# Another order of the first steps in a fused window-attention and MLP kernel

## The chip, the cores and the metric

The kernel runs on one core of a Trainium2 chip. The metric is the device time of one execution in microseconds (us); several executions give a median. One execution is also recorded by the hardware profiler, and its trace is what is read below. The engines are called PE (TensorE, matmuls), DVE (VectorE), ACT (ScalarE), POOL (GpSimd) and SP (SyncE, which here only issues transfers); "PEld" is TensorE's weight load and "POOLq", "SPq", "ACTq" are the issues of transfers on the queues of these engines.

## The reference

An attention with a sliding window and a few sink positions is followed by a two-layer MLP with a rational activation. Cut to what matters:

```python
# q, k, v: (4, 8, 768, 64) float32; n_sink 4, window 128
scores = q @ k.T / sqrt(64), kept where key < 4 or 0 <= query - key < 128
x = softmax(scores) @ v                     # heads side by side: (3072, 512)
h = x @ w_in                                # (3072, 2048)
P = a0 + a1*h + a2*h**2 + a3*h**3
Q = 1 + |b0|*|h| + |b1|*h**2
out = (P / Q) @ w_out                       # (3072, 512)
```

## The kernel before

The work is cut into 12 steps of 256 rows (4 batches of 3 steps). Each step has an attention part and an MLP part. Everything is a named "piece" with an engine; ORDER, a hand-written list of piece numbers, says in which order all pieces are issued, and so each engine's queue: every engine works through its own pieces in that order and waits at the head of its queue until the inputs of the piece are there. ENGINE says for pieces that can go to ScalarE or VectorE which one takes them, BANK which of four PSUM tiles (ps_h, ps_o, ps_m, ps_s, two banks each) a piece writes. Each of these tiles exists once, so a piece that writes ps_h waits until the reader of its previous contents is done.

The pieces, with s the step (or m in the MLP):

- Step 0's k and q: load_k0 and load_q0 (two halves, on the ACT and SP queues, in float32), cast_k0 and cast_q0 (to bf16), turn_k0 and turn_q0 (TensorE transposes into PSUM), place_k0 and place_qc 0 (copies out of PSUM).
- Steps 1 to 3: load_kc and load_qc (POOL's queue, cast in flight), turn_kc and turn_qc, place_kc and place_qc. Steps 0 to 2 have load_vc, turn_vc and place_vc for v in the same way; turn_vc multiplies with the selection tile "sel", which is made of the identity.
- From step 4 on k and q go through POOL's load_k and load_q and through DMA transposes on SP's queue, turn_k and turn_q. v goes through load_v, one for each head.
- scores s i (four parts), exps s i (ScalarE), attend s G (two parts), norm s G (a reciprocal and a multiplication on VectorE), turn_x and placed_x, which give x transposed.
- gemm1 m j (four parts of x @ w_in), copy_in m j (ScalarE), then on VectorE and ScalarE and, sqa or sqd (square), den, ln, exp, even, odd, odd_h, num and gate, then gemm2 m (w_out) and copy_out, store. Step 0 does this chain in four quarters.
- hold x s and hold h m: a one-element copy on POOL that reads the norm of step s (or the hidden rows of step m), so that the loads behind it on POOL's queue are issued only then.
- Small things: "neg" and "edges" (mask tiles), "ident", sink_consts, spread, cast_vs, turn_vs, spread_vs (sink rows of v), babs (on ScalarE) and scale_x and scalars (on VectorE; the norms multiply with what scale_x gives), clear_* and ones_* (fills), spin n (n matmuls of 128 columns on a constant tile, which compute nothing that is used).

The dependency that the list keeps is in the calls of piece(); for example the norm:

```python
piece(("norm", s, G), "DVE", 0.97, 4 * s + at - 5 - 0.1,
      lambda s=s, G=G: normalize(s, G),
      [("attend", s, G), ("scale_x",), ...
```

The order is written out by hand, and the last loop of the kernel issues it:

```python
names = list(work)
for n in ORDER:
    if n < 0:
        spin(-n)
    elif work[names[n]].run:
        work[names[n]].run()
```

Of the kernel before, what the change touches and what calls it, by code (L numbers as in the profile page):

```python
# [61 lines left out]
def kernel(  # L62
# [50 lines left out]
    inv_sqrt_d = 1.0 / float(D) ** 0.5  # L113
    NEG = -30000.0
    PE_MASK = tuple(range(12))
    ENGINE = {('cast_q0', 0): 'DVE',
               ('cast_q0', 1): 'DVE',
               ('place_k0', 1): 'ACT',
               ('place_kc', 2, None): 'ACT',
# [1148 lines left out]
```

## Time and profile before

| | us |
|---|---|
| median of 3 runs | 242.64 (241.71 to 242.86) |
| the profiled execution | 240.56 |
| its span, from the first to the last instruction | 238.9 |

| engine | busy us | share of the span | instructions |
|---|---|---|---|
| PE | 216.1 | 90% | 3229 |
| DVE | 215.2 | 90% | 253 |
| ACT | 210.1 | 88% | 172 |
| POOL | 92.7 | 39% | 126 |

A timeline row gives the start in us, the duration in us, the engine, the line of the kernel, the operation and its tiles, how many instructions are merged in it, and in brackets how long the engine was idle before it and what released it. A row of transfers gives the tile, the queue, the number of issues, the size and the time from the issue to the landing.

### The profile page before, as it was taken

Reading aid. Unit: us, or ns where it says so; the run is one execution under the profiler, and the core shown is the slowest. Engines: PE = TensorE matmul, PEld = TensorE weight load, DVE = VectorE, ACT = ScalarE, POOL = GpSimd, SP = SyncE. Lnnn points to the kernel's source line nnn. Section 1 sums busy time; section 2 is a strip of 40 time slices with the busy share of each in tenths; the row PEclk is TensorE's granted clock in tenths of the full one; section 3 lists DMA queues with packets and bytes.
Section 4 is the critical chain, followed back from the end, with each engine's and each line's share of the span. In section 5 each row is a group of like instructions: output and inputs, shape, how many; then the busy total and the mean of one; then the engine's idle time right before and its main releaser. Section 6 shows DMA issues by size and latency. Waiting matters only on the chain.

```text
span 238.9 us, 7308 instructions
## 1 busy us (share of the span) xinstructions
PE 216.1 (90%) x3229; PEld 146.8 (61%) x3249; DVE 215.2 (90%) x253; ACT 210.1 (88%) x172; POOL 92.7 (39%) x126
## 2 busy tenths in 40 slices
PE   0497898995999999999999999999999999999993
PEld 0365676784874757746578658568647768545431
DVE  3678299999799999898999999999999999999991
ACT  2357799997899998999999899999999999999960
POOL 8914409597939880499910980000000000000000
PEclk9999999999999999999999999999999999999999
DMA  6999999999999999799994999570305110004222
GB/s 186 166 178 137 202 170 79 125 134 128 164 185 147 137 162 150 208 98 77 141 129 89 158 89 73 140 125 26 25 3 198 25 25 0 1 3 170 93 88 88
DMA packets 95375, 26.98 MB, mean 113 GB/s; under 512 B 86128, under 2 KB 92272, under 8 KB 95344
## 3 DMA queue, kind: packets, MB, share of 16 engines
q0 software_dynamic: 65024, 12.98, 84.8%
q1 hardware_dynamic: 28792, 12.61, 28.4%
q10 hardware_dynamic: 1528, 0.93, 1.4%
q8 instruction: 25, 0.41, 0.8%
q14 instruction: 6, 0.05, 0.1%
HBM read 27.30 MB, written 6.29 MB: 141 GB/s over the span
## 4 chain that ended last, share of the span: by engine, by line
PE 52%; ACT 24%; DVE 7%; DMA 6%; issue 4%; POOL 4%; SPq 2%; ACTq 0%; POOLq 0%; DVEq 0%
PE ps_h L829 18%; PE ps_o L767 9%; PE ps_m L767 8%; ACT lnq L811 6%; ACT hb L774 5%; ACT den L816 4%; DMA kT<-k_bf 4%; PE ps_m L829 3%; ACT sq L781 3%; ACT e L667 3%; PE ps_h L767 2%; DMA v<-in_v_dram 2%; PE ps_m L708 2%; PE ps_s L647 1%; SPq L602 1%
## 5 line engine op out<-in xcount | busy, mean ns | idle before, releaser
L767 PEld LDWEIGHTS <-w_in_sb 128*128 128x128 bf16 x768 | 73.7, 98 | 14.8 <-issue 3.5
L829 PE MATMUL ps_h<-w_out_sb,g 128*128 128x512 bf16 x287 | 68.2, 379 | 1.9 <-issue 1.0
L829 PEld LDWEIGHTS <-g 128*128 128x128 bf16 x384 | 36.6, 98 | 42.0 <-DVE g L821 1.6
L811 ACT ACTIVATE lnq<-den,one_eps,qsc 128x4096 f32<-128x4096 bf16 (+1 forms) x18 | 48.2, 2678 | 0.0
L816 ACT ACTIVATE den<-lnq 128x4096 bf16<-128x4096 f32 (+1 forms) x18 | 44.8, 2491 | 0.2
L767 PE MATMUL ps_m<-xblk,w_in_sb 128*128 128x256 bf16 x352 | 42.1, 273 | 0.6 <-ACT hb L774 0.3
L767 PE MATMUL ps_o<-xblk,w_in_sb 128*128 128x256 bf16 x336 | 40.2, 273 | 0.0
L381 POOL DMA_DIRECT2D v<-in_v_dram x48 | 36.1, 765 | 0.1
L808 DVE TENSOR_TENSOR num<-num,sq 128x4096 bf16<-128x4096 bf16 (+1 forms) x18 | 28.3, 1578 | 0.2
L821 DVE TENSOR_TENSOR g<-num,den 128x4096 bf16<-128x4096 bf16 (+1 forms) x18 | 28.3, 1574 | 0.1
L805 DVE TENSOR_TENSOR sq<-sq,hb 128x4096 bf16<-128x4096 bf16 (+1 forms) x18 | 28.3, 1576 | 0.1
L792 DVE TENSOR_TENSOR den<-den,sq 128x4096 bf16<-128x4096 bf16 (+1 forms) x18 | 28.2, 1574 | 0.1
L774 ACT ACTIVATE hb<-ps_o 128x1024 bf16<-128x1024 f32 x21 | 21.8, 1038 | 3.3 <-PE ps_o L767 3.2
L774 ACT ACTIVATE hb<-ps_m 128x1024 bf16<-128x1024 f32 x22 | 22.9, 1039 | 0.6 <-PE ps_m L767 0.5
L667 ACT ACTIVATE e<-ps_s 128x768 bf16<-128x768 f32 (+1 forms) x25 | 22.1, 885 | 0.0
L781 ACT ACTIVATE sq<-hb 128x1024 bf16<-128x1024 bf16 (+1 forms) x15 | 20.1, 1355 | 0.1
L797 DVE TENSOR_SCALAR num<-sq,acoef 128x4096 bf16<-128x4096 bf16 (+1 forms) x18 | 18.3, 1024 | 0.4 <-ACT sq L781 0.3
L801 DVE TENSOR_SCALAR sq<-sq,acoef 128x4096 bf16<-128x4096 bf16 (+1 forms) x18 | 17.9, 999 | 0.2
L783 DVE TENSOR_TENSOR sq<-hb 128x2048 bf16<-128x2048 bf16 (+2 forms) x13 | 16.9, 1300 | 1.0 <-ACT hb L774 0.9
L708 PEld LDWEIGHTS <-e 64*64 64x64 bf16 x1216 | 13.1, 107 | 5.4 <-issue 4.4
L343 POOL DMA_DIRECT2D q_bf<-in_q_dram x15 | 14.8, 988 | 3.7 <-DMA w_out_sb<-in_moe_w_out_dram 3.5
L788 DVE TENSOR_SCALAR den<-hb 128x2048 uint32<-128x2048 uint32 (+1 forms) x18 | 16.1, 896 | 0.0
(136 smaller groups left out, 265.8 us busy)
## 6 DMA issues: line engine op xcount, KB each, us to landing
out_dram<-o_t SPq DMA_DIRECT2D x11, 512.0 KB, 3.0
w_in_sb<-in_moe_w_in_dram POOLq DMA_DIRECT2D x4, 512.0 KB, 10.8
k_bf<-in_k_dram POOLq DMA_DIRECT2D x16, 128.0 KB, 6.2
w_out_sb<-in_moe_w_out_dram POOLq DMA_DIRECT2D x4, 512.0 KB, 8.8
q_bf<-in_q_dram POOLq DMA_DIRECT2D x15, 128.0 KB, 6.2
v<-in_v_dram POOLq DMA_DIRECT2D x24, 64.0 KB, 5.8
stage_v<-in_v_dram POOLq DMA_DIRECT2D x3, 256.0 KB, 9.8
v<-in_v_dram POOLq DMA_DIRECT2D x24, 32.0 KB, 5.0
```

What stands on the lines that cost most here:

```text
L381: nc.gpsimd.dma_start(out=v_fix[b % 2][half(r), g * NHF:(g + steps) * NHF, hl, 0:D], in_=v[b, h, g * TS:(g + steps) * TS, :].rearrange("(j ...
L667: nc.scalar.activation(out=data, in_=ps[:, :, c0:512], func=AF.Exp, scale=inv_sqrt_d)
L767: nc.tensor.matmul(ps[:, n, :], lhsT=w_in_all[:, c, fc * P:(fc + 1) * P], rhs=xblk[m][:, c, :], start=(c == 0), stop=(c == NDMC - 1))
L774: nc.scalar.activation(out=hb[m][:, j * GW:(j + 1) * GW], in_=ps_h.pop((m, j)).rearrange("p n c -> p (n c)"), func=AF.Copy)
L781: nc.scalar.activation(out=sq[m][:, c], in_=hb[m][:, c], func=AF.Square)
L792: nc.vector.tensor_tensor(out=den[m][:, c], in0=den[m][:, c], in1=sq[m][:, c], op=ALU.add)
L805: nc.vector.tensor_tensor(out=sq[m][:, c], in0=sq[m][:, c], in1=hb[m][:, c], op=ALU.mult)
L808: nc.vector.tensor_tensor(out=num[m][:, c], in0=num[m][:, c], in1=sq[m][:, c], op=ALU.add)
L811: nc.scalar.activation(out=lnq_fix[:, c], in_=den[m][:, c], func=AF.Ln, scale=qsc, bias=one_eps)
L816: nc.scalar.activation(out=den[m][:, c], in_=lnq_fix[:, c], func=AF.Exp, scale=-1.0)
L821: nc.vector.tensor_tensor(out=g_of[m][:, c], in0=num[m][:, c], in1=den[m][:, c], op=ALU.mult)
L829: nc.tensor.matmul(ps_out[own][:, tt, :], lhsT=g_of[m][:, co:co + P], rhs=w_out_all[:, fc, :], start=(fc == 0), stop=(fc == NFFC - 1))
```

## The change

ORDER is changed in its first 319 entries; from there on the list is the same. The spin of 3 ahead of the first scores becomes a spin of 7 between the two turns of q for step 3. Eight pieces change their engine and some thirty their PSUM tile. The queues of the engines, written out by names as far as they differ (before, after):

```
PE    before  q0 0, k0 1, q0 1, k0 0 (turns), turn_kc 1, spin 3, scores 0 1, scores 0 2, turn_vs 0, turn_qc 1,
              scores 0 3, scores 0 0, turn_vs 1, turn_vc 0, turn_kc 2, attend 0 1, attend 0 0, turn_vc 1, scores 1 0,
              turn_x 0 1, turn_x 0 0, turn_qc 2, scores 1 3, 1 2, 2 2, 2 0, 1 1, gemm1 0 1, attend 1 0, turn_kc 3,
              turn_vc 2, gemm1 0 2, gemm1 0 0, attend 1 1, scores 2 1, turn_qc 3 1, turn_x 1 0, turn_qc 3 0, scores 2 3, ...
      after   q0 1, q0 0, k0 0, k0 1 (turns), turn_qc 1, scores 0 1, turn_kc 1, scores 0 3, turn_vs 1, scores 0 0,
              turn_vc 0, turn_vc 1, turn_vs 0, scores 0 2, turn_kc 2, scores 1 0, attend 0 1, turn_qc 2, attend 0 0,
              scores 2 2, scores 1 3, turn_x 0 1, scores 2 0, scores 1 2, turn_x 0 0, scores 1 1, gemm1 0 1, attend 1 0,
              scores 2 3, turn_vc 2, turn_kc 3, gemm1 0 2, gemm1 0 0, attend 1 1, turn_qc 3 0, spin 7, turn_qc 3 1, ...
ACT   before  (loads), place_qc 0 0, place_qc 0 1, place_k0 1, exps 0 1, 0 2, 0 3, 0 0, place_vc 0, babs, load_a,
              place_kc 2, place_vc 1, exps 1 0, place_qc 2, exps 1 3, 1 2, 2 2, copy_in 0 1, exps 1 1, 2 0, place_kc 3, ...
      after   (loads), load_a, cast_q0 0, place_qc 0 1, place_k0 0, place_k0 1, place_qc 1, exps 0 1, 0 3, place_kc 1,
              exps 0 0, place_vc 1, exps 0 2, babs, exps 1 0, place_qc 2, exps 2 2, 2 0, 1 3, 1 2, 1 1, copy_in 0 1,
              exps 2 3, place_kc 3, place_vc 2, ...
DVE   before  neg, fills, cast_q0 1, sel, fills, ones_vs, spread, cast_k0 1, sink_edge, cast_q0 0, cast_vs 1, cast_k0 0,
              place_k0 0, cast_vs 0, k_sink 0, place_kc 1, ones_v, spread_vs 0, place_qc 1, spread_vs 1, sink_mask 0,
              scale_x, norm 0 1, norm 0 0, placed_x 0 1, placed_x 0 0, scalars, norm 1 0, ..., place_vc 2, ..., norm 1 1
      after   neg, fills, cast_q0 1, cast_k0 1, ones_vs, sel, cast_k0 0, place_qc 0 0, k_sink 0, sink_edge, spread,
              ones_v, cast_vs 1, spread_vs 1, cast_vs 0, place_vc 0, spread_vs 0, sink_mask 0, scale_x, place_kc 2,
              norm 0 1, norm 0 0, placed_x 0 1, scalars, placed_x 0 0, norm 1 0, ..., norm 1 1
POOL  before  edges, sink_consts, load_kc 1, load_qc 1, ident, load_vc 0, load_kc 2, load_vc 1, load_v 3 4, load_kc 3,
              load_qc 2, load_w_in 1, load_vc 2, hold x 0, load_w_in 2, load_w_in 0, load_qc 3, load_w_in 3, load_v 3 1,
              load_k 4 0, load_k 4 1, hold x 1, load_q 9, load_v 4 1, load_k 5 1, load_v 3 7, load_q 10, load_k 5 0,
              load_v 3 6, load_q 11, hold x 2, ...
      after   sink_consts, ident, edges, load_qc 1, load_kc 1, load_vc 0, load_vc 1, load_kc 2, load_v 3 7, load_qc 2,
              load_kc 3, load_w_in 1, load_vc 2, load_w_in 2, hold x 0, load_w_in 0, load_v 3 4, load_v 3 6, load_qc 3,
              load_w_in 3, load_q 11, load_k 4 0, hold x 1, load_q 10, load_v 4 1, load_q 9, load_k 5 1, load_k 4 1,
              load_v 3 1, load_k 5 0, hold x 2, ...
SP    before  ..., turn_k 4 1, turn_q 9, turn_k 5 1, turn_k 4 0, turn_q 10, turn_q 11, turn_k 5 0, ...
      after   ..., turn_k 4 0, turn_q 10, turn_q 9, turn_k 5 1, turn_k 4 1, turn_q 11, turn_k 5 0, ...
```

The diff, with the first lines of ORDER and all else:

```diff
 ORDER = [
-    3, 108, 126, 1, 2, 125, 128, 109, 117, 127, 113, 118, 0, 14, 15, 146, 107, 110, 5, 4, 16, 119,
-    136, 121, 122, 129, 140, 8, 116, 143, 133, 144, 137, 141, 145, 147, 138, 148, 139, 142, 149,
-    130, 178, -3, 182, 150, 184, 183, 131, 185, 120, 151, 132, 24, 186, 152, 180, 18, 187, 181, 17,
...
+    3, 109, 126, 1, 2, 125, 128, 107, 127, 108, 0, 15, 117, 113, 146, 14, 110, 118, 119, 140, 5,
+    147, 111, 136, 122, 4, 8, 143, 148, 16, 144, 137, 145, 138, 139, 121, 141, 151, 142, 178, 182,
+    152, 116, 129, 149, 120, 133, 27, 183, 186, 134, 17, 187, 180, 135, 150, 18, 6, 181, 101, 9,
...
@@ -113,16 +113,16 @@
     inv_sqrt_d = 1.0 / float(D) ** 0.5
     NEG = -30000.0
     PE_MASK = tuple(range(12))
-    ENGINE = {('cast_q0', 0): 'DVE',
-               ('cast_q0', 1): 'DVE',
+    ENGINE = {('cast_q0', 1): 'DVE',
+               ('place_k0', 0): 'ACT',
                ('place_k0', 1): 'ACT',
-               ('place_kc', 2, None): 'ACT',
+               ('place_kc', 1, None): 'ACT',
                ('place_kc', 3, None): 'ACT',
-               ('place_qc', 0, 0): 'ACT',
                ('place_qc', 0, 1): 'ACT',
+               ('place_qc', 1, None): 'ACT',
                ('place_qc', 2, None): 'ACT',
                ('place_qc', 3, 0): 'ACT',
-               ('place_vc', 2): 'DVE',
+               ('place_vc', 0): 'DVE',
                ('placed_x', 0, 0): 'DVE',
                ('placed_x', 0, 1): 'DVE',
                ('placed_x', 1, 0): 'DVE',
@@ -132,8 +132,7 @@
                ('placed_x', 3, 1): 'DVE',
                ('placed_x', 4, 0): 'DVE',
                ('placed_x', 4, 1): 'DVE'}
-    BANK = {('attend', 0, 0): 'ps_h',
-             ('attend', 0, 1): 'ps_o',
+    BANK = {('attend', 0, 1): 'ps_o',
              ('attend', 1, 1): 'ps_h',
              ('attend', 2, 1): 'ps_o',
              ('attend', 3, 0): 'ps_o',
@@ -186,15 +185,14 @@
              ('gemm1', 11, 3): 'ps_m',
              ('gemm2', 6, 0, 0): 'ps_m',
              ('gemm2', 9, 0, 0): 'ps_o',
-             ('scores', 0, 0): 'ps_h',
-             ('scores', 0, 1): 'ps_m',
+             ('scores', 0, 1): 'ps_s',
              ('scores', 0, 3): 'ps_m',
-             ('scores', 1, 1): 'ps_h',
-             ('scores', 1, 2): 'ps_o',
-             ('scores', 1, 3): 'ps_h',
-             ('scores', 2, 2): 'ps_m',
-             ('scores', 2, 3): 'ps_m',
+             ('scores', 1, 1): 'ps_m',
+             ('scores', 1, 2): 'ps_h',
+             ('scores', 2, 0): 'ps_m',
+             ('scores', 2, 2): 'ps_o',
              ('scores', 3, 0): 'ps_h',
+             ('scores', 3, 2): 'ps_m',
              ('scores', 4, 1): 'ps_h',
              ('scores', 5, 1): 'ps_o',
              ('scores', 5, 2): 'ps_m',
@@ -209,21 +207,21 @@
              ('scores', 10, 2): 'ps_m',
              ('scores', 10, 3): 'ps_o',
              ('scores', 11, 1): 'ps_m',
-             ('turn_k0', 0): 'ps_h',
-             ('turn_kc', 1, None): 'ps_o',
-             ('turn_kc', 2, None): 'ps_h',
+             ('turn_k0', 0): 'ps_o',
+             ('turn_k0', 1): 'ps_h',
+             ('turn_kc', 1, None): 'ps_h',
              ('turn_kc', 3, None): 'ps_o',
-             ('turn_qc', 1, None): 'ps_o',
-             ('turn_qc', 2, None): 'ps_o',
-             ('turn_qc', 3, 0): 'ps_h',
-             ('turn_vc', 1): 'ps_o',
+             ('turn_q0', 1): 'ps_m',
+             ('turn_qc', 2, None): 'ps_h',
+             ('turn_qc', 3, 1): 'ps_h',
+             ('turn_vc', 1): 'ps_h',
              ('turn_vc', 2): 'ps_h',
-             ('turn_vs', 0): 'ps_h',
+             ('turn_vs', 0): 'ps_o',
              ('turn_vs', 1): 'ps_o',
-             ('turn_x', 0, 0): 'ps_h',
-             ('turn_x', 1, 0): 'ps_o',
+             ('turn_x', 0, 0): 'ps_o',
+             ('turn_x', 0, 1): 'ps_h',
              ('turn_x', 1, 1): 'ps_o',
-             ('turn_x', 2, 0): 'ps_o',
+             ('turn_x', 2, 0): 'ps_h',
              ('turn_x', 2, 1): 'ps_h',
              ('turn_x', 3, 1): 'ps_h',
              ('turn_x', 4, 0): 'ps_o',
```

## Rows read from the trace of the kernel before

**Rows 1.** Busy time by stretches: us, PE, PEld, DVE, ACT, POOL, granted clock, DMA.

```profile
28.00:42.00 14.00, 12.52 (x276) 10.04 (x268) 13.16 (x26) 13.94 (x16) 5.76 (x9) 1.00 1.54 133
120.00:160.00 40.00, 39.65 (x691) 27.54 (x695) 39.43 (x35) 39.06 (x31) 11.55 (x15) 1.00 1.22 109
```

**Rows 2.** The chain that ended last, in order of time: start, us, what.

```profile
36.42 0.88 POOL q_bf L343
...
50.32 8.66 DMA kT<-k_bf
```

**Rows 3.** Timeline of the first 6 us, queues of SP and POOL.

```profile
1.75 0.42 SPq L331 DMA_DIRECT2D stage_b<-in_q_dram  x1
...
3.15 1.03 POOL L356 DMA_DIRECT2D stage_d<-in_k_dram  x1
3.69 0.45 SPq L321 DMA_DIRECT2D stage_a<-in_k_dram  x1
...
5.04 0.42 POOL masks.py:197 MEMSET ident<- 128x128 bf16 x1
5.54 0.29 POOL masks.py:199 TENSOR_SCALAR_AFFINE_SELECT ident<-ident 128x128 bf16<-128x128 bf16 x1
```

**Rows 4.** Timeline of 4 to 14 us, DVE, PE and ACT.

```profile
4.50 1.09 DVE L569 CAST early<-stage_b 128x768 bf16<-128x768 f32 x1 [1.55 <-DMA stage_b<-in_q_dram]
...
5.86 0.85 DVE L398 COPY sel<-ident 64x64 bf16<-64x64 bf16 x4
...
9.00 0.82 PE L551 MATMUL ps_h<-ident,early 128*128 128x128 bf16 x6 [9.00 <-DVE early L569]
...
9.07 0.40 DVE L569 CAST early<-stage_a 128x512 bf16<-128x512 f32 x1
...
9.86 0.81 ACT L567 ACTIVATE qT<-ps_h 128x768 bf16<-128x768 bf16 x1 [7.76 <-PE ps_h L551]
...
11.78 1.06 PE L551 MATMUL ps_o<-ident,stage_d 128*64 128x128 bf16 x16 [0.47 <-ACT qT L567]
...
12.88 1.22 DVE L569 COPY kT<-ps_o 128x1024 bf16<-128x1024 bf16 x1
...
13.21 0.53 PE L647 MATMUL ps_m<-qT,kT 64*64 64x192 bf16 x8
```

**Rows 5.** Transfers of step 0 and 1: queue, issues, KB, us to landing.

```profile
stage_b<-in_q_dram SPq DMA_DIRECT2D x1, 384.0 KB, 4.9
...
stage_a<-in_k_dram SPq DMA_DIRECT2D x1, 256.0 KB, 4.2
...
stage_d<-in_k_dram POOLq DMA_DIRECT2D x1, 256.0 KB, 5.7
...
stage_d<-in_q_dram POOLq DMA_DIRECT2D x1, 256.0 KB, 7.2
```

**Rows 6.** Timeline of 18 to 29 us, PE, DVE and ACT.

```profile
18.34 0.64 PE L551 MATMUL ps_h<-ident,stage_d 128*64 128x128 bf16 x16 [0.39 <-ACT e L667]
...
19.82 0.16 DVE L511 TENSOR_TENSOR ratio<-bpos,binv 128x2 f32<-128x2 f32 x1
...
20.23 0.75 DVE L717 SCALAR_TENSOR_TENSOR x_n<-ps_o,ratio,rec 128x512 bf16<-128x512 f32 x1
...
25.99 1.92 PE L767 MATMUL ps_o<-xblk,w_in_sb 128*128 128x256 bf16 x16
...
27.95 1.02 ACT L774 ACTIVATE hb<-ps_o 128x1024 bf16<-128x1024 f32 x1 [1.47 <-PE ps_o L767]
```

**Rows 7.** Timeline of 59 to 72 us, PE.

```profile
59.02 0.36 PE L647 MATMUL ps_m<-qT,kT 64*64 64x192 bf16 x8 [2.44 <-DMA kT<-k_bf]
...
71.26 1.89 PE L829 MATMUL ps_h<-w_out_sb,g 128*128 128x512 bf16 x8
```

**Rows 8.** The loads of w_out: durations and starts of the issues; the last landing.

```profile
L433 POOL DMA_DIRECT2D w_out_sb<-in_moe_w_out_dram x4: 750/761/1368, 50.2 to 60.1; - x4
...
w_out_sb<-in_moe_w_out_dram POOLq DMA_DIRECT2D x1, 512.0 KB, 11.0
```

72 rows, old and new, of the table ORDER are left out of this document.

## The prediction

> **What bounds the kernel now.** I read three views, from the coarse to the fine. First the busy time by stretches: in the middle of the kernel TensorE, VectorE and ScalarE are each busy for over 39 of 40 us, and between 28 and 42 us ScalarE is busy for 13.94 of 14 us, VectorE for 13.16, TensorE for 12.52 [rows 1]. So there is no single bound; the kernel loses time where all three wait, and an edit that only shifts work among them moves the balance. What is left to win lies ahead of 28 us, and in one gap at 59 us. The chain of waits names that gap's cause: POOL starts a run of loads at 36.42 us, right behind the hold on the norm of step 1, and SP's last k turn of step 5 takes 8.66 us from 50.32 us [rows 2]; TensorE goes on at 59.02 us, after 2.44 us of idleness [rows 7]. Last I walked the timeline of the first 28 us. All later queues keep their order, so the question is one number: how much sooner or later than before the engines leave the region that is reordered, at about 42 us.
>
> **The change, part by part.** I walk it with the durations of the timeline, 0.05 us from an end to the start that it releases, and 0.1 us of overlap between neighbours on ScalarE. All times after the change are estimates from these rows.
>
> *POOL.* Before, edges and sink constants come first, the first load issues at 3.15 us, and the identity stands behind two loads, from 5.04 to 5.83 us [rows 3]. After it is constants, identity, edges: the edges, and with them the first load, come 0.8 us later, at 3.9 us. So "neg" (0.6 us) ends on VectorE at 4.6 us, and the first cast starts there instead of at 4.50 us [rows 4]: 0.1 us lost, hidden below. The load of q for step 1 becomes the first load, issued at 3.95 us, k of step 1 the second, at 4.85 us. The trace has no load of that q in first place, so bounds: the first in line took 5.7 us to land, the second 7.2 us [rows 5]. I take the place in line and not the tensor: q lands at 9.65 us (11.15 at the latest), k at 12.05 us (10.55 at the earliest). Behind them the queue moves the same bytes up to w_in 1, at most 0.8 us later than before. Its user, gemm1 0 1, started with no wait on its row [rows 6] behind scores that still stand ahead of it; without that cover it would cost the 0.8 us, I count nothing. w_in 2 moves ahead of the hold on norm 0, its user is later still: nothing.
>
> *First steps.* SP issues its q half (q0 0) at 1.75 us and its k half (k0 0) at 3.69 us [rows 3]; they take 4.9 and 4.2 us [rows 5] and land at 6.65 and 7.9 us. Before, VectorE did all four casts, with the selection tile (a fill and 0.85 us of copies) behind the first, and the first turn started at 9.00 us [rows 4]. After:
> - ScalarE casts q0 0 at its landing, 6.65 us. No such cast stands in the trace; a 768-column pass on ScalarE took 0.81 us, on VectorE as a cast 1.09 us [rows 4]; I take 0.85 us, 7.5 us. load_a, now ahead of it on that queue, is issued while ScalarE waits.
> - VectorE: cast q0 1 to 5.75, cast k0 1, fills, selection tile to 7.9 us, where k0 0 has just landed: cast k0 0 (0.40 us, [rows 4]) to 8.35 us. Then place_qc 0 0 (768 columns; three quarters of the 1.22 us of 1024, [rows 4]: 0.95 us) to 9.3 us.
> - TensorE: turn q0 1 at 5.8, turn q0 0 (0.82 us, [rows 4]) from 7.5 to 8.3, turn k0 0 to 8.95; turn k0 1 needs ps_h, which place_qc 0 0 frees at 9.3 us: to 9.9 us. ScalarE's placements of k0 end at 9.6 and 10.55 us. Turn qc 1 now stands ahead of the first scores: at 9.95 us with q landed, 1.06 us [rows 4], to 11.0 us. Scores 0 1 start at 11.05 us; before it was 13.21 us [rows 4]. The lead here is 2.1 us, and 0.7 us if q lands at its late bound.
>
> *Where the lead goes.* Turn kc 1 waits for k at 12.05 us and ends at 13.15; scores 0 3 to 13.85. ScalarE now also places qc 1 and kc 1, so that its passes follow one another: exps 0 1 (11.95), exps 0 3 (13.9), place kc 1, exps 0 0 (15.5), place vc 1 (16.85), exps 0 2 to 18.55, babs to 18.75. VectorE's scale_x has to wait for babs (three instructions of 0.16 us and their gaps, [rows 6]: 19.35), place_kc 2 is queued behind it (1.22 us, [rows 4]: 20.55), and norm 0 1 behind that: 20.55 to 21.5, norm 0 0 to 22.45 us (a reciprocal of 0.2 and 0.75 us, [rows 6], each). That is later than before, where the multiplication of norm 0 1 began at 20.23 us [rows 6]: the early lead is spent by this point, on VectorE. But TensorE and ScalarE have done more meanwhile. Scores 2 2 need the bank that norm 0 1 frees (21.55), scores 2 0 the one of norm 0 0 (22.95); exps 2 0 end at 24.7, scores 1 1 at 25.25, and gemm1 0 1 starts at 25.3 us instead of 25.99 us [rows 6]. copy_in 0 1 starts on ScalarE at 27.2 us instead of 27.95 us [rows 6], with exps 1 1 and 2 0 done already, where before they followed.
>
> *From 28 to 42 us.* ScalarE is rid of the two exps (1.6 us) and has place_vc 2 (0.9 us) and 0.6 us of new gaps instead, before exps 2 3 and place_kc 3. Its lead stays 0.75 + 1.6 - 0.9 - 0.6 = 0.85 us, and 1.1 us with the small gaps of before closed. VectorE is rid of place_vc 2 (1.2 us): norm 1 1 ends 1.2 us sooner, and the loads behind its hold begin at 35.2 us and not at 36.42 us [rows 2]. The spin of 7 (one 512- and three 128-column matmuls; 0.4 us, by 16 of 256 columns in 1.92 us [rows 6]) stands where TensorE has to wait for norm 1 1 anyway: nothing, and 0.4 us if that wait is gone. That the spin of 3 is gone is in the walk.
>
> *A second sum as a test.* Moved work in whole passes: ScalarE gains a cast, one 512-column and three 1024-column placements (0.85 + 0.6 + 3 x 1.0, by its 0.81 us for 768 columns [rows 4] and 1.02 us for 1024 [rows 6]) and gives away 0.8 + 2 x 1.0: 1.65 us more. It starts 3.2 us sooner (6.65 against 9.86 us, [rows 4]); on my walk it has 1.5 us more idle gaps: a lead of only 0.1 us, and 0.1 us of overlap for each of two added passes: 0.3 us. VectorE gets 2 us less work. Between 0.3 and 1.1 us I take 1.0 us, since the walk knows the order and this sum does not.
>
> *From 42 us on.* The run of loads behind the hold of step 1 starts 1.2 us sooner, and of the SP turns before the last k turn of step 5 one (q 11) no longer waits, since its load goes ahead of that hold. (load_k 4 1 goes behind it; its turn is the fifth on SP, where that of q 10 was fifth, so the scores of step 4 get their last input no later.) SP reaches the k turn at about 47.5 us instead of 50.32 us [rows 2], and the 2.44 us wait at 59 us [rows 7] goes. But this gain isn't kept: the third and fourth quarters of w_out are needed next. The last is issued at 60.1 us and lands 11.0 us later, at 71.1 us [rows 8]; the gemm2 part that reads it starts at 71.26 us [rows 7]. Those loads are queued behind the hold on norm 3, which moves with the engines, by 1.0 us. So TensorE waits there in place of at 59 us, and leaves with the lead of 1.0 us. After that the engines run as densely as in the second row of [rows 1], and a lead is carried to the end.
>
> *The clock.* The column of the granted clock reads 1.00, the level of 2.4 GHz, in both stretches of [rows 1]. Yet the same 16 turns took 1.06 us at 11.78 us and 0.64 us at 18.34 us [rows 4, 6]: TensorE ran slowly in its first 8 us of work. I kept the slow durations up to 16.9 us, as before. The Trainium skill's page "TensorE: Matmul & The Clock Gate" (Part 1: The HAM clock gate) says that the array is throttled by default and that activity releases it. By that rule the order after, which starts TensorE in short bursts with waits between and drops the spin of 3, may stay slow for longer; by it the sum becomes the third rival's. The trace agrees as to the start of the kernel; for gaps in it no row shows it.
>
> **The rivals.**
> 1. *The gain at 59 us is kept.* For it: the w_out loads share their queue with loads that would finish sooner once the turns are out of their way. Against: the last landing and its user lie 0.16 us apart [rows 7, 8]. If w_out follows half of the way, the lead is 1.0 + 0.5 x 2.44, and with the closing of gaps on the others up to 2.6 us: 240.0 us.
> 2. *Nothing is left.* The landing of k for step 1 is 1 us later than I take it (13.05 us, 8.2 us from its issue), or ScalarE's extra 1.65 us binds from 28 us on, where it had no idle time to give [rows 1]. Lead 0: 242.6 us.
> 3. *Slower, by the clock.* If TensorE stays at the slow rate until gemm1 0 1 is done, by the ratio 1.06 to 0.64 of [rows 4, 6] the five scores behind norm 0 and two turns cost some 1.2 us more in all, and gemm1 0 1 (1.92 us, [rows 6]) 1.3 us more: 2.5 us against the lead of 1.0 us, 244.1 us. It decides from the point where the slow rate lasts to about 25 us.
>
> **How the numbers follow.** The profiled execution took 240.56 us for a span of 238.9 us; the sum makes it 239.6 us. The runs shown have a median of 242.64 us, 2.1 us above it, and I keep that distance: 241.6 us. A change of under 0.5%, 1.2 us here, can't be told from none. Chances: forecast 0.46 (own range 240.7 to 242.3 us, by leads of 0.3 to 1.9 us; 0.20 of it beyond 1.2 us), first rival 0.20, second 0.18, third 0.16. Faster: 0.20 + 0.20 = 0.40. Slower: the third and 0.02 of the second, 0.18. The same: 0.42. The range of 239.8 to 243.6 us takes in the first rival's time and half of the third's stretch; 2 in 10 are left out.
>
> **What would show it.** The first scores near 11 us behind a turn of qc 1; ScalarE's cast near 6.7 us; VectorE idle ahead of scale_x near 18.7 us; norm 0 1 later than before, but gemm1 0 1 near 25.3 us; the hold of step 1 near 35 us; no kT wait near 56 us, but TensorE waiting for w_out_sb near 69 us. I am wrong if TensorE's turns of 16 still take 1.06 us after 18 us, if turn qc 1 waits past 11 us for its q, or if the wait for w_out_sb is missing and the end is 2 us or more sooner.

## The result

The changed kernel takes 238.03 us (median of 6 runs, 237.24 to 242.69); the kernel before 241.59 us (median of 6 runs, 239.89 to 242.86, three of them those that I started from). The ratio is 0.9894, 95% interval 0.9853 to 0.9936: faster by 1.1%, about 2.6 us, while the two medians lie 3.6 us apart. I had forecast 241.6 us, a gain of 1.0 us. Of the 3.6 us between forecast and median, 1.05 us is the kernel before, whose median of six is that much below the one that I started from; the rest, 2.5 us by the medians and 1.6 us by the ratio, is gain that I did not see.

The ratio leaves out executions that are long for their kernel, and the first profiled execution of the changed kernel was one of these (span 241.0 us), so the rows below are of another execution of the same kernel, 237.63 us with a span of 235.9 us, 3.0 us shorter than the span before. In that first execution TensorE waited for kT even longer than before, and the granted clock fell to 0.50 behind the wait:

```profile
51.82 1.92 PE L765 MATMUL ps_m<-xblk,w_in_sb 128*128 128x256 bf16 x16
...
58.78 0.54 PE L645 MATMUL ps_m<-qT,kT 64*64 64x192 bf16 x8 [3.54 <-DMA kT<-k_bf]
```

So what follows is what the changed kernel can do, not what it does each time. In the changed kernel the line numbers are lower by 2 (L827 is the L829 of before).

The timeline of TensorE, ScalarE and VectorE in the first 14 us, which answers to [rows 4]:

```profile
4.56 0.69 DVE L567 CAST early<-stage_b 128x768 bf16<-128x768 f32 x1 [0.18 <-DMA stage_b<-in_q_dram]
...
5.30 0.82 PE L549 MATMUL ps_m<-ident,early 128*128 128x128 bf16 x6 [5.30 <-DVE early L567]
...
6.67 0.35 ACTq L940 DMA_DIRECT2D a_bc<-in_moe_a_dram  x1
7.07 0.84 ACT L565 ACTIVATE early<-stage_b 128x768 bf16<-128x768 f32 x1 [4.98 <-DMA stage_b<-in_q_dram]
...
10.37 1.06 PE L549 MATMUL ps_m<-ident,stage_d 128*64 128x128 bf16 x16
...
11.37 0.53 PE L645 MATMUL ps_s<-qT,kT 64*64 64x192 bf16 x8
```

The first turn starts at 5.30 us instead of 9.00, the first scores at 11.37 instead of 13.21. The same timeline from 14 to 37 us, with TensorE, VectorE, ScalarE and POOL, answers to [rows 6] and to the hold of [rows 2]:

```profile
14.70 0.63 PE L408 MATMUL ps_m<-stage_v,sel 64*64 64x256 bf16 x16
...
17.20 0.64 PE L549 MATMUL ps_m<-ident,stage_d 128*64 128x128 bf16 x16
...
20.16 0.75 DVE L715 SCALAR_TENSOR_TENSOR x_n<-ps_o,ratio,rec 128x512 bf16<-128x512 f32 x1
...
24.19 1.94 PE L765 MATMUL ps_o<-xblk,w_in_sb 128*128 128x256 bf16 x16
...
26.16 1.02 ACT L772 ACTIVATE hb<-ps_o 128x1024 bf16<-128x1024 f32 x1 [0.32 <-PE ps_o L765]
...
29.72 0.71 PE L765 MATMUL ps_o<-xblk,w_in_sb 128*128 128x256 bf16 x5
...
31.52 1.37 PE L765 MATMUL ps_o<-xblk,w_in_sb 128*128 128x256 bf16 x11 [1.09 <-issue]
...
35.15 0.88 POOL L341 DMA_DIRECT2D q_bf<-in_q_dram  x1
```

gemm1 0 1 starts at 24.19 us, 1.80 us ahead of before. Then 1.09 us of it is lost inside gemm1 0 0. From 48 us on, SP's and POOL's queues and TensorE (answering to [rows 2, 7, 8]):

```profile
48.38 1.22 SPq L604 DMA_TRANSPOSE kT<-k_bf  x1
...
49.72 0.82 POOL L431 DMA_DIRECT2D w_out_sb<-in_moe_w_out_dram  x1
...
52.35 1.92 PE L765 MATMUL ps_m<-xblk,w_in_sb 128*128 128x256 bf16 x16
...
55.60 0.34 PE L645 MATMUL ps_m<-qT,kT 64*64 64x192 bf16 x8
56.08 1.92 PE L765 MATMUL ps_h<-xblk,w_in_sb 128*128 128x256 bf16 x16
...
68.09 1.89 PE L827 MATMUL ps_h<-w_out_sb,g 128*128 128x512 bf16 x8
```

The scores that waited 2.44 us for kT at 59.02 us [rows 7] now start at 55.60 us with no wait on their row. And 12 us later nothing waits for w_out: the part of gemm2 that started at 71.26 us [rows 7] starts at 68.09 us. Which quarters of w_out a part reads is in the calls of piece(): gemm2 0 has four parts of 8 matmuls, and TensorE takes 0 0 0 and 0 1 0 first, which depend on load_w_out 0 and 1, and then 0 1 1 and 0 0 1, which depend on load_w_out 2 and 3. The part at 71.26 us is 0 1 0. The parts that need the last quarter come next, before and after, and with them the landing of the second quarter before:

```profile
73.98 3.63 PE L829 MATMUL ps_h<-w_out_sb,g 128*128 128x512 bf16 x15
...
70.82 3.63 PE L827 MATMUL ps_h<-w_out_sb,g 128*128 128x512 bf16 x16
...
w_out_sb<-in_moe_w_out_dram POOLq DMA_DIRECT2D x1, 512.0 KB, 7.8
```

The loads of w_out in the changed kernel, by the line of their issues, then the third by itself and the last by itself:

```profile
L431 POOL DMA_DIRECT2D w_out_sb<-in_moe_w_out_dram x4: 750/794/1374, 49.7 to 59.1; - x4
...
w_out_sb<-in_moe_w_out_dram POOLq DMA_DIRECT2D x1, 512.0 KB, 8.8
...
w_out_sb<-in_moe_w_out_dram POOLq DMA_DIRECT2D x1, 512.0 KB
```

The last is issued at 59.1 us, 1.0 us sooner than before. The 8.8 us are those of the third load; the landing of the last isn't recorded in this trace (runs 3 and 6 have it). The starts of gemm1 and gemm2 in both traces give the lead at each point:

| TensorE starts | before | after | lead, us |
|---|---|---|---|
| gemm1 0 1 | 25.99 | 24.19 | 1.80 |
| gemm1 1 1 | 44.41 | 43.94 | 0.47 |
| last gemm1 ahead of the kT wait | 53.16 | 52.35 | 0.81 |
| gemm1 2 0, behind it | 59.42 | 56.08 | 3.34 |
| gemm2 0 1 0 | 71.26 | 68.09 | 3.17 |
| gemm2 0 1 1, the last quarter | 73.98 | 70.82 | 3.16 |
| last gemm2 | 233.95 | 231.00 | 2.95 |

So in this pair of traces the reordered steps themselves leave 0.8 us, near the 1.0 us that I had walked out. The other 2.5 us come at 56 to 59 us, from the wait that I expected to go, and they are kept.

### The profile page after: what moved, and what is told of

Same layout as the page of the kernel before. It is cut to its first block, busy times and chain, and to the rows that moved or that the text cites. A ratio compares the mean times of both kernels' runs of the same rounds, so it can differ in the third digit from the quotient of the medians.

```text
span 241.0 us, 7312 instructions
## 1 busy us (share of the span) xinstructions
PE 218.3 (91%) x3230; PEld 147.2 (61%) x3250; DVE 213.5 (89%) x251; ACT 212.2 (88%) x174; POOL 91.1 (38%) x126
## 4 chain that ended last, share of the span: by engine, by line
PE 54%; ACT 20%; DMA 9%; DVE 8%; issue 4%; SPq 3%; POOL 1%; ACTq 0%; DVEq 0%
PE ps_h L827 17%; PE ps_o L765 11%; PE ps_m L765 9%; ACT lnq L809 5%; ACT hb L772 5%; DMA kT<-k_bf 4%; PE ps_m L827 3%; ACT e L665 3%; PE ps_h L765 3%; ACT den L814 3%; DMA q_bf<-in_q_dram 3%; ACT sq L779 2%; DMA stage_b<-in_q_dram 2%; DVE g L819 2%; PE ps_m L706 2%
## 5 line engine op out<-in xcount | busy, mean ns | idle before, releaser
L765 PEld LDWEIGHTS <-w_in_sb 128*128 128x128 bf16 x768 | 74.7, 99 | 17.4 <-issue 5.0
L827 PE MATMUL ps_h<-w_out_sb,g 128*128 128x512 bf16 x287 | 68.2, 379 | 1.9 <-issue 1.0
L827 PEld LDWEIGHTS <-g 128*128 128x128 bf16 x384 | 36.5, 98 | 42.1 <-DVE g L819 1.6
L765 PE MATMUL ps_o<-xblk,w_in_sb 128*128 128x256 bf16 x336 | 41.2, 276 | 0.7 <-issue 0.7
L379 POOL DMA_DIRECT2D v<-in_v_dram x48 | 35.4, 750 | 4.9 <-DVE sink_rows L447 4.3
L665 ACT ACTIVATE e<-ps_s 128x768 bf16<-128x768 f32 (+1 forms) x27 | 23.7, 877 | 0.6 <-PE ps_s L653 0.6
L795 DVE TENSOR_SCALAR num<-sq,acoef 128x4096 bf16<-128x4096 bf16 (+1 forms) x18 | 18.9, 1057 | 0.4 <-ACT sq L779 0.2
L799 DVE TENSOR_SCALAR sq<-sq,acoef 128x4096 bf16<-128x4096 bf16 (+1 forms) x18 | 18.4, 1030 | 0.2
L781 DVE TENSOR_TENSOR sq<-hb 128x2048 bf16<-128x2048 bf16 (+2 forms) x13 | 16.9, 1299 | 0.8 <-ACT hb L772 0.8
L372 POOL DMA_DIRECT2D k_bf<-in_k_dram x16 | 15.1, 950 | 5.3 <-DMA kT<-k_bf 4.2
```

The costliest lines, as they stand in the source:

```text
L379: nc.gpsimd.dma_start(out=v_fix[b % 2][half(r), g * NHF:(g + steps) * NHF, hl, 0:D], in_=v[b, h, g * TS:(g + steps) * TS, :].rearrange("(j ...
L665: nc.scalar.activation(out=data, in_=ps[:, :, c0:512], func=AF.Exp, scale=inv_sqrt_d)
L765: nc.tensor.matmul(ps[:, n, :], lhsT=w_in_all[:, c, fc * P:(fc + 1) * P], rhs=xblk[m][:, c, :], start=(c == 0), stop=(c == NDMC - 1))
L827: nc.tensor.matmul(ps_out[own][:, tt, :], lhsT=g_of[m][:, co:co + P], rhs=w_out_all[:, fc, :], start=(fc == 0), stop=(fc == NFFC - 1))
```

## The experiments

Ratios are against the kernel before on the same chip. Orders are written by the names of the pieces.

**1. The changed kernel again**, for a profile and a second ratio (no edit).

> The changed kernel once more, unedited. Theory A (the first steps give a lead of about 2 us on all engines by 40 us, and it is carried to the end): 2 to 2.5 us under the kernel before (ratio 0.990), gemm1 0 1 near 24.0 us and gemm1 1 0 near 38.1 us in the trace, against 25.99 and 40.18 us before. Theory B (the gain comes from the loads of step 4 and 5, so that the wait for kT near 59 us goes): the same ratio, but a trace in which TensorE's wait for kT is under 0.5 us. If TensorE waits over 3 us for kT there and its granted clock falls behind the wait, the gain is lost again (about 241 us).

238.87 us, ratio 0.9894 [0.9825, 0.9962]. The profile above is its. TensorE waits neither for kT nor, near 68 us, for w_out: theory B's sign. Of theory A's lead of 2 us by 40 us 0.47 us are there at gemm1 1 1.

**2. The kernel before with the late loads of the change**

```diff
 POOL: ..., load_vc 2, hold x 0,
-      load_w_in 2, load_w_in 0, load_qc 3, load_w_in 3, load_v 3 1, load_k 4 0, load_k 4 1, hold x 1, ...
+      load_w_in 0, load_v 3 4, load_v 3 6, load_qc 3, load_w_in 3, load_q 11, load_k 4 0, hold x 1, ...
 SP:
-      turn_k 4 1, turn_q 9, turn_k 5 1, turn_k 4 0, turn_q 10, turn_q 11, turn_k 5 0
+      turn_k 4 0, turn_q 10, turn_q 9, turn_k 5 1, turn_k 4 1, turn_q 11, turn_k 5 0
```

> The kernel before, with only the loads from the hold on the norm of step 0 on (POOL's queue) and the turns of SP in the order of the changed kernel. Theory A: no difference that can be told (ratio 0.997 to 1.003), the wait for kT near 59 us stays at 2 to 3 us. Theory B: 1.5 to 2.5 us under the kernel before (0.990 to 0.994) and the wait for kT under 0.5 us.

240.44 us, 0.9992 [0.9944, 1.0039]: no gain that can be told. Yet its trace has no wait for kT, which theory A didn't expect. It is of an execution in which the granted clock fell to 0.50 from 21 to 24 us; w_out's first load comes at 51.44 us there, the last k turn at 49.94.

**3. The changed kernel with the late loads of before** (the reverse edit).

> The changed kernel, with the loads behind the hold on the norm of step 0 and the turns of SP put back to the order before. Theory A: ratio 0.989 to 0.992, as the changed kernel. Theory B: 0.997 to 1.003.

238.03 us, 0.9892 [0.9832, 0.9953], and no wait for kT in its trace: the whole gain. So the new order of the loads isn't needed for it; the first steps are enough. Here the landing of w_out's last quarter is recorded, and the row that reads it:

```profile
w_out_sb<-in_moe_w_out_dram POOLq DMA_DIRECT2D x1, 512.0 KB, 11.3
...
71.47 3.63 PE L827 MATMUL ps_h<-w_out_sb,g 128*128 128x512 bf16 x16
```

The quarter is issued at 59.2 us and takes no less than before (11.0 us): it lands at 70.5 us, 1.0 us ahead of its reader, and nothing waits.

**4. The changed kernel with the k of step 5 still earlier**

```diff
 POOL: ..., load_k 4 0,
+      load_k 5 0, load_k 5 1,
       hold x 1, ...
 SP:   turn_k 4 0,
+      turn_k 5 0, turn_k 5 1,
       turn_q 10, ...
```

> The changed kernel, with both loads of k for step 5 ahead of the hold on the norm of step 1 and their turns second and third among SP's turns of step 4 and 5, so that kT of step 5 lands some 10 us sooner. Theory A with the cap as I predicted it (the last quarter of w_out lands too late): the wait for kT goes, TensorE waits for w_out near 69 us instead, the time is that of the changed kernel within 0.5 us. Rival (nothing waits there): 2 to 3 us under the changed kernel, ratio to the kernel before 0.978 to 0.983.

238.72 us, 0.9919 [0.9882, 0.9955]. Both k turns of step 5 are issued by 40.7 us (the one at 45.73 us is step 4's). TensorE waits neither for kT nor for w_out, whose last quarter takes 10.8 us to land, but idles 1.53 us ahead of an attend at 44.18 us. So neither the cap that I had predicted nor the rival's 2 to 3 us shows: with the wait gone there is nothing more to win from an earlier turn.

**5. The kernel before again**, one execution.

> The kernel before once more, unedited, for a second trace. Theory C (the wait for kT near 59 us is a race: SP issues the last k turn of step 5 just behind POOL's first load of w_out, 50.32 against 50.16 us, and the turn's packets then share the DMA engines with that load): the wait is there again, 1 to 2.5 us, the turn issued behind the w_out load. Theory D (the wait is a chance event of the one profiled execution): no wait over 0.5 us, and a span of about 237 us.

241.22 us. TensorE waits 2.10 us for kT, and in SP's and POOL's rows the last k turn stands again just behind the first load of w_out:

```profile
50.51 1.22 SPq L606 DMA_TRANSPOSE kT<-k_bf  x1
...
50.16 0.76 POOL L433 DMA_DIRECT2D w_out_sb<-in_moe_w_out_dram  x1
```

**6. The kernel before with the first load of w_out later**

```diff
 POOL: ..., six load_v,
-      load_w_out 0, hold h 0, four load_v, hold h 1, ...
+      hold h 0, four load_v, load_w_out 0, hold h 1, ...
```

> The kernel before, with one edit: the load of the first quarter of w_out is issued four v loads later on POOL's queue (about 54 us instead of 50.2 us). Theory C: the turn lands 5 to 6 us after its issue and not 8.7, the wait for kT is under 0.5 us, and the time falls by 1 to 2 us (ratio 0.992 to 0.996), less where w_out then lands too late for gemm2. Theory D: ratio 0.998 to 1.002.

239.97 us, 0.9959 [0.9926, 0.9992]. The wait for kT is gone with this one load moved; gemm1 2 0 starts at 56.88 us (59.42 before) and gemm2 0 1 0 at 68.72 us (71.26). So the gain passes w_out in full here too, with the last quarter landing as late as before:

```profile
w_out_sb<-in_moe_w_out_dram POOLq DMA_DIRECT2D x1, 512.0 KB, 10.9
...
71.44 3.63 PE L829 MATMUL ps_h<-w_out_sb,g 128*128 128x512 bf16 x15
```

Issued at 60.3 us, it lands at 71.2 us, 0.3 us ahead of its reader. Half of the gain is lost later: TensorE waits 1.1 us for xblk<-x_n, which it didn't before, and the span is 237.7 us.

**7. The changed kernel with that load three v loads earlier.**

> The changed kernel, with one edit: the load of the first quarter of w_out is issued three v loads earlier on POOL's queue (about 47.5 us, ahead of the last k turn of step 5). Theory C: the wait for kT comes back, 2 to 3 us, and most of the gain goes (ratio to the kernel before 0.996 to 1.002). Theory D: ratio 0.988 to 0.991, as the changed kernel.

244.8 us, 1.0152 [1.0092, 1.0212]: slower by more than the change had won, but by another wait than expected. The longest waits of TensorE from 40 to 66 us:

```profile
PE ps_h L706 <- DMA v<-in_v_dram: 4.5, 1, 4.5
PE ps_m L765 <- DVE x_n L715: 0.8, 1, 0.8
```

The v loads now stand behind 512 KB on their own queue, and attend waits for v before kT can show. Theory C named the wrong victim.

**8. The kernel before with TensorE kept busier in the first steps**

```diff
 PE:   ..., turn_kc 2,
+      spin 4,
       attend 0 1,
+      spin 4,
       attend 0 0,
+      spin 4,
       turn_vc 1, ...
```

> The kernel before, with three spins of one 512-column matmul each, ahead of attend 0 1, attend 0 0 and turn_vc 1, where TensorE had gaps between 18 and 22 us. Theory E (part of the gain of the changed kernel is that its denser TensorE queue keeps the granted clock up near 21 us, where another run with the first steps of the kernel before fell to 0.50 for 3.5 us): the granted clock stays at 1.00 to 40 us in the trace, and the median of the fast executions falls by 0.5 to 1.2 us (ratio 0.995 to 0.998). Without theory E: ratio 1.000 to 1.003, by the work added.

240.16 us, 0.9954 [0.9915, 0.9993]. In its trace the granted clock stays at 1.00 through the first steps, as theory E had it, and TensorE still waits 1.66 us for kT. The mean granted clock was above 0.9935 in 8 of 10 executions.

**9. The changed kernel with the later w_out of run 6.**

> The changed kernel with the first quarter of w_out loaded four v loads later, right ahead of the hold on h of step 1, the edit that gave the kernel before 0.9959. Theory C (the changed kernel owes part of its gain to the last k turn of step 5 getting ahead of w_out; the first steps' lead already puts it ahead, by 0.8 to 1.3 us): nothing to win in its undisturbed executions, ratio 0.985 to 0.991, with less scatter, since the executions in which w_out came first (a wait of 3.5 us for kT) are gone. Rival F: w_out's packets slow the earlier turns and v loads as well, so that the later load wins again: ratio 0.980 to 0.985. Rival G: w_out now lands too late and TensorE waits for it near 68 us: 0.992 to 0.998.

238.64 us, 0.9933 [0.9895, 0.9971]: nothing won. The ratio lies in the range that rival G named, but TensorE waits nowhere for w_out (0.5 us in two waits for v is all that is new), so G isn't shown; C's range was too low, and run 11 beside it has 0.9919. All 12 executions have a mean clock of 0.998 or more.

**10. The kernel before with the edits of runs 6 and 8 together.**

> The kernel before with two edits together that gave it 0.9959 and 0.9954 alone: w_out's first quarter behind four more v loads, and three spins of TensorE in the first steps. It has none of the change's first steps. Theory C+E (the two causes are separate and their sum is most of the change's gain): 0.989 to 0.993, within 0.3% of the changed kernel. Rival H (both removed the same wait, or the first steps' lead is needed as well): 0.994 to 0.997.

240.27 us, 0.9979 [0.9943, 1.0016]. The two gains don't add, and my sum C+E fell. In the trace gemm1 0 1 starts later, with the spins ahead of it (26.65 us), the k turn goes at 50.96 us, and TensorE waits 1.25 us for kT although w_out comes 3 us behind the turn.

**11. The changed kernel with the cast of q0 0 back on VectorE**

```diff
-    ENGINE = {('cast_q0', 1): 'DVE',
+    ENGINE = {('cast_q0', 0): 'DVE',
+               ('cast_q0', 1): 'DVE',
```

> The changed kernel with the cast of q0 0 back on VectorE, ahead of the cast of k0 0: the one part of the change that names an engine. It takes the cast of 0.84 us off ScalarE and gives VectorE some 0.7 us ahead of the first turns. By the prediction's walk (the first turns set the first scores, but the lead is spent on VectorE by norm 0 1): first scores up to 0.7 us later, the time within 0.3 us of the changed kernel, ratio 0.988 to 0.992. Rival: every part of the lead of 0.8 us comes from the cast on ScalarE, w_out gets ahead of the last k turn again and TensorE waits 2 us for kT: 0.996 to 1.001.

238.68 us, 0.9919 [0.9883, 0.9955]. The first scores start at 11.57 us, 0.2 us later, the last k turn at 48.49 us, and no wait for kT: this part is worth nothing that can be measured.

**12. The kernel before, for its clock**, one execution.

> The kernel before, unchanged, once more, for its clock alone. Of 71 executions of it beside the earlier runs, 44 had a mean granted clock of 0.9935 or less, and these have a median span of 240.05 us where the other 27 have 238.6 us; the two traces of it so far are both of the full clock. Theory E (the fall lies in the first steps, as in the kernel with late loads, whose first steps are the same): with about 6 chances in 10 the mean clock is below 0.9935, and then the granted clock falls to about 0.5 between 20 and 26 us, gemm1 0 1 starts 0.5 to 1.3 us later than 25.99 us, and the rest of the span is at 1.00. Rival: the fall lies behind the wait for kT at 59 us.

239.59 us, mean clock 0.993. The busy time of the engines by stretches, with the granted clock third from the end:

```profile
18.00:19.00 1.00, 0.28 (x31) 0.28 (x35) 0.97 (x5) 1.00 (x4) 0.00 (x0) 1.00 1.31 221
19.00:20.00 1.00, 0.77 (x70) 0.62 (x57) 0.80 (x4) 0.47 (x1) 0.00 (x0) 1.00 1.23 192
20.00:21.00 1.00, 0.06 (x5) 0.00 (x0) 0.33 (x1) 0.00 (x0) 0.55 (x2) 0.89 1.63 175
21.00:22.00 1.00, 0.87 (x18) 0.74 (x17) 0.54 (x2) 0.00 (x0) 1.00 (x2) 0.50 1.21 106
22.00:23.00 1.00, 1.00 (x28) 0.49 (x20) 0.42 (x1) 0.63 (x1) 1.00 (x3) 0.50 0.63 64
23.00:24.00 1.00, 1.00 (x16) 0.74 (x8) 0.09 (x1) 1.00 (x2) 1.00 (x3) 0.50 1.19 193
24.00:25.00 1.00, 0.83 (x20) 0.57 (x22) 1.00 (x5) 0.66 (x2) 1.00 (x2) 0.91 1.16 185
```

TensorE had been idle for 0.85 us and then 1.07 us, and the clock fell to 0.50, the level of 1.2 GHz, until past 24 us. gemm1 0 1 starts at 26.97 us, 0.98 us later. What follows I hadn't expected: w_out's first load waits for the hold and moves from 50.16 to 51.15 us, the last k turn goes at 50.69 us, and the wait for kT is gone; the span is 237.9 us, 1.0 us under that of the first trace.

**13. The changed kernel with its lead taken back**

```diff
 PE:   ..., gemm1 0 2, gemm1 0 0,
+      spin 20,
       attend 1 1, ...
```

> The changed kernel with a spin of 20 on TensorE (five 512-column matmuls, about 1.07 us by its spins) ahead of attend 1 1 at 32.8 us, which takes back the lead of 1.06 us that it has there, and nothing else. Theory C (the lead alone puts the last k turn of step 5 early enough): the hold on the norm of step 1 is back near 35.6 us, the last k turn near 49.4 us, the wait for kT of 1 to 2.5 us is back, and the end loses 1.5 to 3 us: ratio 0.995 to 1.002. Rival I (the order of the queues after the change keeps the turn clear of w_out, whatever the lead): no wait for kT, at most the delay of 1.0 us is lost, ratio 0.990 to 0.994.

239.85 us, 0.9967 [0.9921, 1.0013]. SP's and POOL's queues, then TensorE:

```profile
50.63 1.22 SPq L604 DMA_TRANSPOSE kT<-k_bf  x1
...
50.54 0.82 POOL L431 DMA_DIRECT2D w_out_sb<-in_moe_w_out_dram  x1
...
60.03 0.53 PE L645 MATMUL ps_m<-qT,kT 64*64 64x192 bf16 x8 [2.93 <-DMA kT<-k_bf]
60.71 3.60 PE L765 MATMUL ps_h<-xblk,w_in_sb 128*128 128x256 bf16 x16
```

The turn falls behind w_out and the wait returns, as theory C has it and against I. But the first profile of the unedited changed kernel shows the same, a turn behind w_out and a wait of 3.54 us, with nothing taken back. And the ratio's interval reaches into the range of rival I. So run 13 doesn't show that it is the lead. The expected places of hold and turn (35.6 and 49.4 us) were met by the hold (35.47), while the turn was 1.2 us later still.

**The place of the last k turn in all traces.** Start of the last k turn of step 5 on SP, of w_out's first load on POOL, and TensorE's wait for kT:

| kernel | turn | w_out | wait, us |
|---|---|---|---|
| before | 50.32 | 50.16 | 2.44 |
| before again (5) | 50.51 | 50.16 | 2.10 |
| spins (8) | 51.58 | 51.12 | 1.66 |
| after, first profile | 49.30 | 49.19 | 3.54 |
| lead taken back (13) | 50.63 | 50.54 | 2.93 |
| before, clock fallen (12) | 50.69 | 51.15 | none |
| late loads (2) | 49.94 | 51.44 | none |
| w_out later (6) | 49.62 | 53.02 | none |
| after (1) | 48.38 | 49.72 | none |
| first steps (3) | 48.77 | 49.22 | none |
| k of step 5 early (4) | by 40.7 | 50.42 | none |
| after, w_out later (9) | 48.87 | 53.16 | none |
| cast on VectorE (11) | 48.49 | 49.15 | none |
| both edits on before (10) | 50.96 | 53.94 | 1.25 |

All five that issue the turn behind the load wait, eight of nine that issue it ahead don't. (Run 7 isn't in the table: its turn at 48.72 us is behind w_out at 47.83, and the wait for v covers whatever kT would have cost.) So a few tenths of a us on two queues go with 1.7 to 3.5 us on TensorE; that the order is the cause rests on run 6, which moves this one load alone.

## Why the prediction was wrong, step by step

*POOL.* Right in kind: the first load goes at 3.53 us (I had 3.9), the second at 4.55 us.

*First steps.* Right. q0 1 is cast at 4.56 us; the cast takes 0.69 us and not the 1.09 us of [rows 4], so the first turn starts at 5.30 us (5.8). ScalarE's cast starts at 7.07 us instead of 6.65, since load_a is issued at 6.67 us ahead of it; it takes 0.84 us (0.85). Turn qc 1 starts at 10.37 us (9.95), scores 0 1 at 11.37 us (11.05), turn kc 1 at 12.04 us, where I had k's landing at 12.05.

*Where the lead goes.* Its place was right and its size off. VectorE does hold up norm 0 1, whose multiplication starts at 20.16 us, as late as before (20.23). But the walk was too long at each hand-over: babs ends 0.47 us ahead of it (18.28 against 18.75 us), norm 0 0 0.64 us (21.81 against 22.45), exps 2 0 0.97 us (23.73 against 24.7), and gemm1 0 1 starts at 24.19 us, 1.1 us ahead of my 25.3.

*The clock.* The third rival pointed at the wrong kernel. I kept TensorE's slow durations up to 16.9 us; in the trace of the changed kernel the last of them is at 13.36 us, in that of run 9 at 14.76 us (16 matmuls of 256 columns in 0.86 us, 0.63 us at full speed). Yet gemm1 0 1 starts at 24.19 and 24.09 us in the two, so TensorE's speed there decided nothing that shows: it is VectorE and ScalarE that it waits for. A loss by the clock in the first steps is found in the kernel before (below).

*From 28 to 42 us.* Here a term was missing. In gemm1 0 0 TensorE stops for 1.09 us, up to 31.52 us, behind five of its 16 matmuls. It isn't w_in that it waits for: the load that this group needs is issued at 21.21 us and takes 8.1 us to land, so it is there before the group starts at 29.72 us:

```profile
w_in_sb<-in_moe_w_in_dram POOLq DMA_DIRECT2D x1, 512.0 KB, 8.1
```

The row's "issue" says that the profile shows nothing that it waits for. Between 29.0 and 31.5 us the trace has one transfer of 0.02 MB on the queue that it calls instruction, as it has ahead of the like stops of runs 2, 4 and 12 (1.40, 1.53 and 1.07 us); that TensorE waits for its own instructions there is inferred. The stop takes back what the walk had missed, and the lead falls to 0.47 to 0.81 us. My 1.0 us was near, out of two errors of opposite sign. The loads behind the hold begin at 35.15 us, as I had it (35.2).

*From 42 us on.* The last k turn of step 5 goes at 48.38 us (I had 47.5), and the wait for kT is gone, as forecast; so it is in runs 3, 4 and 11, while the first profile of the changed kernel still has it. By what it goes I can't say. The order of the loads isn't needed (run 3 has the old one and no wait). The lead alone doesn't do it either: in that first profile it was larger, 1.34 us at the last gemm1 ahead of the kT wait (51.82 us against 53.16) where the trace above has 0.81 us, and yet the turn fell behind w_out. What the lead moves is w_out's first load, which stands 2.63 us ahead of that gemm1 in both (49.19 and 49.72 us). The turn stands 2.52 us ahead of it in the one and 3.97 us in the other, and in the kernel before 2.84 and, with the clock fallen (run 12), 3.46 us: its place depends on SP's earlier turns, and which comes first differs between executions of one kernel.

The step that failed is the next: "But this gain isn't kept: the third and fourth quarters of w_out are needed next." I set the landing of the last quarter, 71.1 us, against the part of gemm2 that starts at 71.26 us [rows 7, 8] and called that part its reader. It isn't. It reads the first two quarters, the second of which lands at 65.8 us (issued at 57.97, 7.8 us); the last quarter is first read at 73.98 us, 2.9 us behind its landing. So the 0.16 us between the two rows were no bound, and w_out had room for the 2.44 us of the kT wait. With that wait out of the way gemm2 0 1 0 followed by 3.2 us, in run 6 by 2.5 us with the first steps of before. The landing didn't become shorter for it: 11.3 us in run 3, 10.8 in run 4, 10.9 in run 6. The first rival had the outcome, by half of the way and with 0.20 of the chances, but not the reason: it reckoned with loads that finish sooner. My sign of being wrong, no wait for w_out_sb and an end 2 us or more sooner, is what came.

*What remains open.* The kernel before had a mean granted clock of 0.9935 or less in 48 of the 83 executions that ran beside the experiments; the changed kernel, with runs 3, 9 and 11, which keep its first steps, in 4 of 38. In the traces of runs 2 and 12 (mean clock 0.993) the fall lies near 21 us, in the first steps that the change rewrites; in the one trace of the four (the first profile, 0.986) it lies behind the wait for kT. So the mean clock alone doesn't tell which fall it was, and how much of the 2.6 us is owed to the first kind can't be split off: in run 12 it costs 0.98 us at gemm1 0 1, and the 2.44 us at 59 us are gone with it. Nor do three traces of the kernel before and two of the changed one, unedited, say how often each has the wait. Why a turn behind w_out's first load lands so late (8.66 us [rows 2]) wasn't measured by itself. The Trainium skill's page "DMA: Bandwidth & Descriptors" (Queues, rings and completion order) says that each transfer engine takes turns between its queues packet by packet; by that a turn would share the engines with w_out and not stand behind all of it. The traces agree: from 52 to 58 us, with w_out under way (q0) and SP's last turn issued (50.32 us before, 48.38 after), the queue of SP's turns (q1) goes on in the kernel before (first two rows) and is done in the changed one (last row):

```profile
q0 software_dynamic: 1733, 0.67, 136.5%
q1 hardware_dynamic: 603, 0.14, 26.5%
...
q0 software_dynamic: 2751, 0.78, 226.1%
```

Run 10, with its wait of 1.25 us though w_out comes 3 us behind the turn, shows that the order alone isn't everything.

## What to carry to other kernels

Before you say that a gain is only passed on to the next transfer, look up in the kernel which instruction reads that transfer: a row that starts just behind a landing need not be its reader. Look for two queues whose issues fall within a few tenths of a us of each other, a small transfer that TensorE needs soon and a big one that it needs late; which goes first can be worth more than the change that shifts them. And try the order by itself, since one moved load (run 6) showed more than the whole reordering. Take more than one trace of a kernel before you call a wait there or gone.

## What the runs showed of the hardware

A wait of 3 us cost more than itself. In run 13 TensorE does 0.10 us of work from 57 to 58 us and none from 58 to 60, the granted clock falls to 0.50, and stays there beyond 64 us:

```profile
57.00:58.00 1.00, 0.10 (x4) 0.00 (x0) 0.96 (x3) 0.96 (x1) 0.55 (x2) 1.00 2.04 167
58.00:59.00 1.00, 0.00 (x0) 0.00 (x0) 1.00 (x2) 0.00 (x0) 1.00 (x2) 0.83 4.66 90
59.00:60.00 1.00, 0.00 (x0) 0.00 (x0) 1.00 (x2) 0.00 (x0) 1.00 (x2) 0.50 4.60 70
60.00:62.00 2.00, 1.97 (x19) 1.27 (x20) 1.68 (x1) 0.81 (x1) 2.00 (x3) 0.50 2.76 104
62.00:64.00 2.00, 2.00 (x11) 1.45 (x10) 0.00 (x0) 0.00 (x0) 2.00 (x4) 0.50 1.23 180
64.00:66.00 2.00, 2.00 (x14) 1.51 (x13) 0.00 (x0) 1.66 (x2) 1.19 (x2) 0.63 1.07 150
```

gemm1 2 0 takes 3.60 us there instead of 1.92, and the next gemm1 2.60 us: with the 2.93 us of waiting, 5.3 us in one place. The wait of 2.44 us in the kernel before left the clock at 1.00. The Trainium skill's page "TensorE: Matmul & The Clock Gate" (Part 1: The HAM clock gate) says that an idle array falls back to half its clock; runs 12 and 13 agree. At the start of the kernel the column reads 1.00 while matmuls run more slowly (1.06 us at 10.37 us for what takes 0.64 us at 17.20 us), so there the durations show what the column doesn't.
